# Chunk-select attention and a squared-relu FFN on one core: ones first, split transposes, codes by DMA, an earlier FFN start

## The chip, the cores and the metric

One core of one Trainium2 chip. The metric is the time of one execution in device microseconds (us). The kernel before took 318.02 us, the median of three runs (317.7 to 319.29).

## The reference

Attention over 4 batches, 8 heads, 768 positions of 64 elements, in which each query sees only the six chunks of 32 keys that have the highest upper bounds; its output, as 3072 tokens of 512, goes through an FFN.

```python
k_min = np.min(k_chunks, axis=3)          # chunks of 32 keys, 24 of them
k_max = np.max(k_chunks, axis=3)
ub = np.sum(np.maximum(q[:, :, :, None, :] * k_min[:, :, None, :, :],
                       q[:, :, :, None, :] * k_max[:, :, None, :, :]), axis=-1)
ub = np.where(causal, ub, -1000000000.0)
top_chunks = np.argsort(ub, axis=-1)[..., -top_k:]      # top_k = 6
scores = scale * np.matmul(q, k.transpose(0, 1, 3, 2))
mask = sel & (pos[:, None] >= pos[None, :])             # selected chunk and causal
attn = softmax(np.where(mask, scores, -1e9))
x = (attn @ v) as 3072 tokens x 512
h = np.maximum(x @ w_in, 0.0)                           # 512 x 2048
out = h * h @ w_out                                     # 2048 x 512
```

## The kernel before, in words

The work is cut into 32 slots: batch, half of its positions (384), pair of heads. Half-batch hb is slots 4 hb to 4 hb + 3; slots 0 to 3 are the first half of batch 0, slots 4 to 7 its second half. A half of kind 0 attends to its own 384 keys, one of kind 1 to all 768. For each slot s the program issues these steps, and one step of a slot stands between steps of its neighbours so that each engine's list (made in program order) is interleaved by hand:

- **T(s)** (step_T, L181): for half-batches 0 to 2, PE transposes the pair's keys and queries (L193) into one PSUM tile; ScalarE (ACT) makes relu(-q) and relu(q) (qr, L197, L198), VectorE (DVE) the chunk minima and maxima of the keys (extrema, L170 to L172, into kbd) and copies keys and queries to the tile kq (place, L213). From half-batch 3 on, DMA transposes on SP's queue do this (tr, place_dma); DVE makes the relus (L235, L236) and step_K the extrema of a half-batch, as a tree of pairwise minima or maxima (L252). step_P picks the way.
- **U(s)** (step_U): upper bounds ub as matmuls of qr with kbd (L280), the eight largest by MAX8 (L287), and a comparison that marks the chunks not selected (L288).
- **V(s)** (step_V): PE transposes the marks (qt, L304, L316); copies put them beside the queries (L309, L310, L320, L321). The keys' side of kq holds a large negative one-hot code of each key's chunk, written once per batch tile and half by codes (L141); a marked chunk thus gets a large negative score.
- **E(s)** (step_E): scores ps (L334), exp on ScalarE (L339), the causal mask of the diagonal blocks on GpSimd (POOL, affine_select, L343).
- **F(s)** (step_F): outputs po = e times v with a column of ones for the sum (L359), its reciprocal (L368), x (L369).
- **X(hb)** (step_X): x transposed (by PE, L385, for hb 0, 1 and the last; by DMA otherwise), then sixteen FFN units "up" (ffn_up: ph, L411; relu ht, L418; square h, L420) and twelve units "down" (ffn_down: py, L430) of the half-batch before are put in a queue. fill and f1 take units from it between the steps of later slots; quota says how many a slot takes.

Loads from HBM are issued by POOL (load_n L84, load_0 L91, load_v L96, w_in L453, w_out L458): half-batch 0's keys and queries and half of V at the start, the others at the end of a slot by the table later (at, go). The keys and queries of head pair 0 come by SP and ACT into staged tiles (L105), are cast by DVE and ACT (L177, L179) and are the first that PE transposes. POOL's list is in order, and loads and masks share it. The loads take eight semaphores, DMASW0 to DMASW7, in turn, and a load waits until the load eight before it has landed.

V's tile vn holds the ones (L132 for batch tile 0, in clear for tile 1). PSUM pools: psS three banks (ps), psF two (ph and T of slots 0 to 5), psY one (py and T of slots 6 to 9), psA two (att: ub, qt, po, pt and T of slots 10, 11).

The start reads:

```python
nc.vector.memset(qn0[:, :, :, 3, :], 0.0)
nc.vector.memset(vn[0][:, :, :, D:D + 1], 1.0)      # L132
...
step_cast()
go(-1, 99)
step_P(0)
```

Of the kernel before, what the change touches and what calls it, by code (L numbers as in the profile page):

```python
# [32 lines left out]
def kernel(  # L33
# [175 lines left out]
    def place(s, h, copy):  # L209
        b, half, p = slots[s]  # L210
        x = st[s]["tkq"]
        n = 1 if s < NP else 2
        copy(kqs[b % 2][h][QROW[h]:QROW[h] + D, p, 2 * half:2 * half + n, :],  # L213
             x[D * h:D * h + D, 0:n, :])
# [44 lines left out]

    def step_P(s):  # L260
        hb = s // NP
        if hb >= ON_PE:
# [1 line left out]
        elif s < NP + 2:
            step_T(s, psF, "ph")
        elif s < 2 * NP + 2:
            step_T(s, psY, "py")
        else:
            step_T(s, psA, "att")
# [235 lines left out]
    nc.vector.tensor_scalar_mul(
        oneh.rearrange("p (c j) -> p c j", j=CH),
        ident[0:D, 0:NC].unsqueeze(2).to_broadcast([D, NC, CH]), OFFSEL)
    place(0, 1, nc.scalar.copy)
# [3 lines left out]
    step_P(1)  # L512
    for s in range(NP):
# [11 lines left out]
        if s == NP - 1:
            step_F(s, 0)
            step_F(s, 1)
            early.close()
            late = ctx.enter_context(tc.tile_pool(name="late", bufs=2))
            step_X(0, True)  # L530
            fill(1, True)
        step_V(s + 1, True)
        step_P(s + 2)
        go(s, 99)
    for s, (b, half, p) in enumerate(slots):
# [14 lines left out]

        f1()
# [77 lines left out]
```

## Time and profile before

| | us |
|---|---|
| median of the runs (317.7, 318.02, 319.29) | 318.02 |
| the profiled execution, own time | 319.25 |
| its span in the profile | 317.6 |
| PE busy | 261.5 (82%) |
| ScalarE (ACT) busy | 180.5 (57%) |
| VectorE (DVE) busy | 173.5 (55%) |
| GpSimd (POOL) busy | 100.5 (32%) |

The profiled execution lies 1.65 above its span and 1.23 above the median. Busy time is a sum over the whole span; where time is lost is read from the timeline and from what ended each idle stretch ("[3.36 <-DVE nsel L288]": idle for 3.36 us until VectorE's line 288 was done). PE's own idle time is 317.6 - 261.5 = 56.1 us, and the page's slices show it mostly in the first fifth.

### The profile page before, as it was taken

Reading aid. Unit: us, or ns where it says so; the run is one execution under the profiler, and the core shown is the slowest. Engines: PE = TensorE matmul, PEld = TensorE weight load, DVE = VectorE, ACT = ScalarE, POOL = GpSimd, SP = SyncE. Lnnn points to the kernel's source line nnn. Section 1 sums busy time; section 2 is a strip of 40 time slices with the busy share of each in tenths; the row PEclk is TensorE's granted clock in tenths of the full one; section 3 lists DMA queues with packets and bytes.
Section 4 is the critical chain, followed back from the end, with each engine's and each line's share of the span. In section 5 each row is a group of like instructions: output and inputs, shape, how many; then the busy total and the mean of one; then the engine's idle time right before and its main releaser. Section 6 shows DMA issues by size and latency. Waiting matters only on the chain.

```text
span 317.6 us, 6256 instructions
## 1 busy us (share of the span) xinstructions
PE 261.5 (82%) x2284; PEld 161.2 (51%) x2284; DVE 173.5 (55%) x637; ACT 180.5 (57%) x387; POOL 100.5 (32%) x142
## 2 busy tenths in 40 slices
PE   0147584978598796989997989989979999999994
PEld 0035452656454464656554556655545666655541
DVE  1176558788667752576348525764476455242321
ACT  2046825687466474776564866776556767744300
POOL 8309526965434132442331314511121111000000
PEclk9999998799799999999999999999999999999999
DMA  9997999999958289699698199993650300000011
GB/s 111 166 78 49 78 180 180 115 105 106 120 38 128 53 83 138 53 192 138 92 139 153 54 148 86 136 162 78 109 133 36 83 2 35 33 35 34 33 68 66
DMA packets 109567, 30.36 MB, mean 96 GB/s; under 512 B 99808, under 2 KB 106464, under 8 KB 109536
## 3 DMA queue, kind: packets, MB, share of 16 engines
q0 software_dynamic: 77280, 13.44, 61.0%
q1 hardware_dynamic: 31456, 16.33, 22.8%
q8 instruction: 18, 0.29, 0.4%
q10 hardware_dynamic: 800, 0.20, 0.3%
q14 instruction: 13, 0.11, 0.1%
HBM read 27.26 MB, written 6.29 MB: 106 GB/s over the span
## 4 chain that ended last, share of the span: by engine, by line
PE 56%; DVE 19%; ACT 9%; issue 7%; DMA 6%; SPq 1%; POOL 1%; ACTq 0%; POOLq 0%; DVEq 0%
PE py L430 21%; PE ph L411 19%; PE ps L334 7%; DVE km L252 5%; PE po L359 4%; DMA xT<-x 4%; ACT e L339 3%; DMA w_in<-in_moe_w_in_dram 2%; DVE kq L213 2%; DVE h L420 2%; SPq L395 1%; DVE km L170 1%; PE ub L280 1%; ACT ht L418 1%; DVE km L171 1%
## 5 line engine op out<-in xcount | busy, mean ns | idle before, releaser
L339 ACT ACTIVATE e<-ps 128x512 bf16<-128x512 f32 x192 | 96.6, 550 | 25.9 <-PE ps L334 25.0
L411 PE MATMUL ph<-xT,w_in 128*128 128x384 bf16 x512 | 104.1, 330 | 6.7 <-DMA xT<-x 4.2
L430 PE MATMUL py<-w_out,h 128*128 128x512 bf16 x384 | 96.6, 379 | 0.0
L420 DVE TENSOR_TENSOR h<-ht 128x384 bf16<-128x384 bf16 x128 | 50.8, 401 | 82.5 <-ACT ht L418 82.3
L418 ACT ACTIVATE ht<-ph 128x384 bf16<-128x384 f32 x124 | 61.1, 496 | 53.6 <-PE ph L411 51.8
L343 POOL TENSOR_SCALAR_AFFINE_SELECT e<-e 128x384 bf16<-128x384 bf16 x64 | 33.9, 531 | 166.7 <-ACT e L339 166.6
L411 PEld LDWEIGHTS <-w_in 128*128 128x128 bf16 x512 | 47.5, 99 | 38.7 <-issue 8.1
L334 PE MATMUL ps<-kq 128*128 128x384 bf16 (+2 forms) x320 | 60.2, 294 | 2.1 <-ACT e L339 1.9
L430 PEld LDWEIGHTS <-h 128*128 128x128 bf16 x384 | 35.7, 98 | 31.3
L334 PEld LDWEIGHTS <-kq 128*128 128x128 bf16 x320 | 28.4, 102 | 16.7 <-issue 1.6
L359 PEld LDWEIGHTS <-e 128*128 128x128 bf16 x672 | 27.2, 100 | 8.8 <-issue 2.3
L359 PE MATMUL po<-vn,e 128*128 128x65 bf16 x672 | 28.8, 198 | 1.7 <-DVE r L368 1.0
L280 PE MATMUL ub<-kbd,qr 128*128 128x48 bf16 (+1 forms) x160 | 9.8, 182 | 14.0 <-DVE qr L235 7.5
L287 DVE MAX8 m<-ub 128x8 f32<-128x24 f32 (+1 forms) x160 | 16.6, 169 | 7.1 <-PE ub L280 7.0
L84 POOL DMA_DIRECT2D kn<-in_k_dram x21 | 18.7, 891 | 0.0
L84 POOL DMA_DIRECT2D qn<-in_q_dram x21 | 18.6, 891 | 0.0
L369 DVE TENSOR_TENSOR x<-po,r 128x384 bf16<-128x384 f32 x32 | 17.8, 557 | 1.1
L193 PE MATMUL tkq<-ident,kn 128*128 128x128 bf16 x36 | 5.5, 281 | 14.0 <-DVE kn L177 14.0
L280 PEld LDWEIGHTS <-qr 128*128 128x128 bf16 x160 | 7.9, 99 | 17.0 <-DVE qr L235 8.7
L436 ACT COPY ob<-py 128x512 f32<-128x512 f32 x18 | 10.7, 593 | 8.5 <-PE py L430 8.3
L316 PE MATMUL qt<-ident,nsel 128*128 128x128 bf16 x72 | 9.1, 229 | 6.7 <-DVE nsel L288 6.7
L170 DVE TENSOR_REDUCE km<-tkq 128x12 bf16<-128x384 bf16 x12 | 6.7, 557 | 14.1 <-ACT qr L198 13.4
(64 smaller groups left out, 191.7 us busy)
## 6 DMA issues: line engine op xcount, KB each, us to landing
out_dram<-ob SPq DMA_DIRECT2D x24, 256.0 KB, 2.2
kq<-kqT SPq DMA_DIRECT2D x10, 384.0 KB, 6.7
vn<-in_v_dram POOLq DMA_DIRECT2D x8, 384.0 KB, 7.5
kn<-in_k_dram POOLq DMA_DIRECT2D x21, 128.0 KB, 4.7
qn<-in_q_dram POOLq DMA_DIRECT2D x21, 128.0 KB, 5.6
w_in<-in_moe_w_in_dram POOLq DMA_DIRECT2D x4, 512.0 KB, 7.6
w_out<-in_moe_w_out_dram POOLq DMA_DIRECT2D x2, 1024.0 KB, 14.0
kn<-in_k_dram POOLq DMA_DIRECT2D x3, 96.0 KB, 3.8
```

The costliest lines, as they stand in the source:

```text
L84: nc.gpsimd.dma_start(out=t.rearrange("p (h d) -> p h d", d=D), in_=(q if n == "q" else k)[b, :, 128 * j:128 * (j + 1)] .rearrange("h p d ...
L280: nc.tensor.matmul(ub[:, j - j0], lhsT=st[s]["qr"][:, w, 128 * j:128 * (j + 1)], rhs=kbds[b % 2][:, p, w, :, 0:ncs], start=False, stop=(j ...
L287: nc.vector.max(out=m8[:, j, hh, :], in_=ub[:, j - j0, hh, :])
L334: nc.tensor.matmul(ps[:, at:at + 128 * m], lhsT=kqs[b % 2][hh][:, p, 2 * (j // HT), 128 * (j % HT):128 * (j % HT + 1)], rhs=qc(s, hh)[:, c ...
L339: nc.scalar.activation(e[:, 512 * n + lo:512 * n + hi], ps[:, lo:hi], ACT.Exp, scale=float(scale))
L343: nc.gpsimd.affine_select(out=d, in_=d, compare_op=ALU.is_ge, fill=0.0, base=0, channel_multiplier=-1, pattern=[[0, 3], [1, 128]])
L359: nc.tensor.matmul(po[:, hh, i, :], lhsT=t["e"][hh][:, c:c + 128], rhs=vn[b % 2][:, 2 * p + hh, j, :], start=(j == 0), stop=(j == iq))
L369: nc.vector.tensor_mul(x[:, :, 128 * p:128 * (p + 1)].rearrange("p j (h d) -> p h j d", h=2), po[:, :, :, 0:D], r.to_broadcast([128, 2, HT ...
L411: nc.tensor.matmul(ph[:, 0:HB], lhsT=w_in[:, ki, 128 * f:128 * (f + 1)], rhs=xT[:, ki, :], start=(ki == 0), stop=(ki == NKI - 1))
L418: nc.scalar.activation(ht, ph[:, 0:HB], ACT.Relu)
L420: nc.vector.tensor_mul(h, ht, ht)
L430: nc.tensor.matmul(py[t], lhsT=h2[hb, f][:, 128 * t:128 * (t + 1)], rhs=w_out[:, f, :], start=(f == 0), stop=(f == NFI - 1))
```

## The change

1. The ones of both V tiles and the zeros of nsel are written by DVE ahead of everything else that it does at the start; the two zero stripes of kq tile 1 are written by DVE at slot 1 and no longer by POOL.
2. kq is one tile per batch parity, not one per head, so that V(s) in slots 0 to 3 is one DVE copy of both heads. In the other slots both copies are DVE's (before, ScalarE made the second one in halves of kind 0).
3. step_T is cut in two: transposes into separate PSUM tiles for keys and queries (different pools for slots 0 to 9) and step_T2 with relus, extrema and placing. For slots 0 to 5 the transposes stand a pair ahead, before F and V of the earlier slot. For slots 4 to 11 DVE places the keys and ScalarE the queries.
4. Codes of (tile 0, half 1) and (tile 1, both halves) are written by six DMAs on SP's queue, not by ScalarE (slot 1) and POOL (slots 4, 5). ScalarE makes the one-hot tile first of all.
5. Loads: half-batch 1's keys and queries and the second half of V right at the start, then all of w_in, half-batch 2, w_out, V of batch 1.
6. step_K: minima at the second slot of a half-batch, maxima at the third (before, both at the third).
7. The FFN starts in slot 4, behind E(4,0): F(3), X(0) and the first units; of half-batch 0's relus every second is DVE's (before, every fourth).

```diff
-    kqs = [[consts.tile([128, NP, 4, HB], BF16, tag=f"kq{i}_{h}", name="kq") for h in range(2)]
-           for i in range(2)]
+    kqs = [consts.tile([128, 2, NP, 4, HB], BF16, tag=f"kq{i}", name="kq") for i in range(2)]
...
+    for i in range(2):
+        nc.vector.memset(vn[i][:, :, :, D:D + 1], 1.0)
     ident = consts.tile([128, 128], BF16, tag="ident")
...
-    nc.vector.memset(vn[0][:, :, :, D:D + 1], 1.0)
+    for i in range(3):
+        nc.vector.memset(nsel[i], 0.0)
...
+    def step_T2(s):
+        b, half, p = slots[s]
+        t = st[s]
         qr = t["qr"] = work.tile([128, 2, HB], BF16, tag="qr", bufs=3, name="qr")
         c = 128 * (1 - half)
-        nc.scalar.activation(qr[:, 0, c:], x[:, 1, c:], ACT.Relu, scale=-1.0)
-        nc.scalar.activation(qr[:, 1, c:], x[:, 1, c:], ACT.Relu)
-        extrema(x[:, 0, :], s)
-        t["tkq"] = x
-        place(s, 0, nc.vector.tensor_copy)
+        nc.scalar.activation(qr[:, 0, c:], t["q"][:, c:], ACT.Relu, scale=-1.0)
+        nc.scalar.activation(qr[:, 1, c:], t["q"][:, c:], ACT.Relu)
+        extrema(t["k"], s)
         if s >= NP:
-            place(s, 1, nc.vector.tensor_copy)
+            place(s, "k", nc.vector.tensor_copy)
+            place(s, "q", nc.scalar.copy)
...
+        step_T(s, *((F, Y) if s < NP + 2 else (Y, A) if s < 2 * NP + 2 else (A, A)))
+        if s >= NP + 2:
+            step_T2(s)
...
-            nc.vector.tensor_copy(qc(s, 0), qt[:, 0])
-            nc.scalar.copy(qc(s, 1), qt[:, 1])
+            nc.vector.tensor_copy(kqs[b % 2][:, :, p, 2 * half + 1, :], qt)
...
-        if hb == 0 and f % 4 == 3:
+        if hb == 0 and f % 2:
...
+    for x in load_half(1):
+        at(-1, *x)
+    at(-1, load_v, 0, 4, 8)
+    for g in range(4):
+        at(0, load_w_in, 512 * g, 512 * g + 512)
+    at(0, codes, 0, 1, nc.sync.dma_start)
+    at(1, clear)
+    for x in load_half(2):
+        at(1, *x)
     for g in range(2):
-        at(-1, load_w_in, 512 * g, 512 * g + 512)
-    at(-1, load_v, 0, 4, 8)
-    at(0, clear)
-    for i, x in enumerate(load_half(1)):
-        at(i // 3, *x)
-    for g in range(2, 4):
-        at(2, load_w_in, 512 * g, 512 * g + 512)
+        at(2, load_w_out, 8 * g, 8 * g + 8)
+    for half in range(2):
+        at(2, codes, 1, half, nc.sync.dma_start)
     for g in range(2):
-        at(3, load_w_out, 8 * g, 8 * g + 8)
-    at(1, codes, 0, 1, nc.scalar.copy)
-    at(4, codes, 1, 0, nc.gpsimd.tensor_copy)
-    at(5, codes, 1, 1, nc.gpsimd.tensor_copy)
-    for x in load_half(2):
-        at(4, *x)
-    for g in range(2):
-        at(5, load_v, 1, 4 * g, 4 * g + 4)
+        at(3, load_v, 1, 4 * g, 4 * g + 4)
...
+        if s == NP:
+            for n in range(hf):
+                step_E(s, 0, n)
+            step_F(s - 1, 0)
+            step_F(s - 1, 1)
...
+            step_X(0, True)
+            quota[0] = 3
         f1()
...
         if ON_PE - 1 <= hb < 2 * B - 1:
-            if p == 2:
-                step_K(hb + 1, 0)
-                step_K(hb + 1, 1)
+            if p == 1 or p == 2:
+                step_K(hb + 1, p - 1)
```

How the order moves, in two places. First DVE's list at the start of the program, before, with what each row waits for; kn0 is the key tile of half-batch 0, stage the staged loads, and DMAHW and DMASW are semaphores of loads:

```order
L130 MEMSET qn_79 128x12x32
L131 MEMSET qn_79 128x12x32
L132 MEMSET vn_73 128x48 [waits DMASW6_49]
L177 CAST kn0_85<-stage_92 128x3x128 [waits DMAHW3_49,DMAHW1_49]
L170 TENSOR_REDUCE km_152<-tkq_142 128x12 [waits PE_49,Activation_49]
```

and DVE's list at the same place now:

```order
L109 MEMSET vn_73 128x48
L109 MEMSET vn_74 128x48
L118 MEMSET cmask_110 128x72
...
L134 MEMSET nsel_87 128x192
L176 CAST kn0_83<-stage_90 128x3x128 [waits DMAHW3_49,DMAHW1_49]
L169 TENSOR_REDUCE km_166<-tk_155 128x12 [waits PE_49]
```

The ones of V no longer stand between the other constants and the cast, and no longer wait for a load of V (DMASW6).

Second, POOL's list from the loads at the end of slot 1 to slot 3, before; e are the masks, two a slot, here of slots 2 and 3:

```order
L84 DMA qn_342<-in_q_dram 128x8x64 [waits DMASW7_49]
L343 AFFINE_SELECT e_346<-e_346 128x3x128 [waits Activation_49]
L343 AFFINE_SELECT e_355<-e_355 128x3x128 [waits Activation_49]
L453 DMA w_in_135<-in_moe_w_in_dram 128x4x512 [waits DMASW0_49]
L453 DMA w_in_135<-in_moe_w_in_dram 128x4x512 [waits DMASW1_49]
L343 AFFINE_SELECT e_421<-e_421 128x3x128 [waits Activation_49,Pool_49]
L343 AFFINE_SELECT e_430<-e_430 128x3x128 [waits Activation_49,Pool_49]
L458 DMA w_out_136<-in_moe_w_out_dram 128x8x512 [waits DMASW2_49]
L458 DMA w_out_136<-in_moe_w_out_dram 128x8x512 [waits DMASW3_49]
```

and now, from the last loads of half-batch 2 on:

```order
L83 DMA qn_352<-in_q_dram 128x8x64 [waits DMASW5_49]
L83 DMA qn_354<-in_q_dram 128x8x64 [waits DMASW6_49]
L83 DMA qn_356<-in_q_dram 128x8x64 [waits DMASW7_49]
L353 AFFINE_SELECT e_358<-e_358 128x3x128 [waits Activation_49,Pool_49]
L353 AFFINE_SELECT e_367<-e_367 128x3x128 [waits Activation_49,Pool_49]
L468 DMA w_out_138<-in_moe_w_out_dram 128x8x512 [waits DMASW0_49]
L468 DMA w_out_138<-in_moe_w_out_dram 128x8x512 [waits DMASW1_49]
L353 AFFINE_SELECT e_440<-e_440 128x3x128 [waits Activation_49,Pool_49]
L353 AFFINE_SELECT e_449<-e_449 128x3x128 [waits Activation_49,Pool_49]
```

Loads of half-batch 2 and w_out have moved ahead of the masks of slots 2 and 3. Counted eight back in the new list of loads, DMASW5 stands for the second half of V, DMASW6 and 7 for the first and the second w_in load, DMASW0 and 1 for the third and the fourth.

## Rows read from the trace of the kernel before

**Rows 1.** The page, part 4: the chain that ended last, share of the span by line.

```profile
PE py L430 21%; PE ph L411 19%; PE ps L334 7%; DVE km L252 5%; PE po L359 4%; DMA xT<-x 4%; ACT e L339 3%; DMA w_in<-in_moe_w_in_dram 2%; DVE kq L213 2%; DVE h L420 2%; SPq L395 1%; DVE km L170 1%; PE ub L280 1%; ACT ht L418 1%; DVE km L171 1%
```

**Rows 2.** Timeline, 0 to 20: start, length, engine, line, operation [idle before <-releaser].

```profile
5.71 0.86 POOL L91 DMA_DIRECT2D qn<-in_q_dram  x1
6.53 1.46 POOL L96 DMA_DIRECT2D vn<-in_v_dram  x1
13.35 0.60 DVE L177 CAST kn<-stage 128x384 bf16<-128x384 f32 x1 [10.41 <-issue]
...
19.81 1.23 PE L334 MATMUL ps<-kq 128*128 128x384 bf16 x5
```

**Rows 3.** DMA issues of 6.5 to 7.9 and of 26 to 27: KB, us to landing.

```profile
vn<-in_v_dram POOLq DMA_DIRECT2D x1, 384.0 KB, 6.7
qn<-in_q_dram POOLq DMA_DIRECT2D x1, 96.0 KB, 3.8
...
kn<-in_k_dram POOLq DMA_DIRECT2D x1, 128.0 KB, 3.5
```

**Rows 4.** Timeline, 26 to 62, of POOL, PE and DVE.

```profile
26.40 2.65 POOL L84 DMA_DIRECT2D kn<-in_k_dram  x3
...
35.91 0.52 POOL L343 TENSOR_SCALAR_AFFINE_SELECT e<-e 128x384 bf16<-128x384 bf16 x1 [0.88 <-ACT e L339]
36.45 0.34 PEld L193 LDWEIGHTS <-qn 128*128 128x128 bf16 x2 [0.40 <-DMA qn<-in_q_dram]
...
41.02 1.78 POOL L458 DMA_DIRECT2D w_out<-in_moe_w_out_dram  x2
41.70 0.82 PE L359 MATMUL po<-vn,e 128*128 128x65 bf16 x12 [1.04 <-DVE r L368]
...
45.70 0.53 PE L316 MATMUL qt<-ident,nsel 128*128 128x128 bf16 x3
46.63 0.81 PE L411 MATMUL ph<-xT,w_in 128*128 128x384 bf16 x4
...
50.45 3.12 POOL L141 COPY kq<-oneh 64x1536 bf16<-64x1536 bf16 x2
50.83 2.94 DVE L420 TENSOR_TENSOR h<-ht 128x384 bf16<-128x384 bf16 x2
...
54.91 0.50 PE L316 MATMUL qt<-ident,nsel 128*128 128x128 bf16 x3 [3.36 <-DVE nsel L288]
...
56.59 1.49 PE L411 MATMUL ph<-xT,w_in 128*128 128x384 bf16 x4
...
57.87 1.06 PE L334 MATMUL ps<-kq 128*128 128x384 bf16 x4
```

**Rows 5.** Timeline, 62 to 100: PE before the transposes of x of half-batch 1.

```profile
84.03 0.77 PE L385 MATMUL pt<-ident,x 128*128 128x128 bf16 x6 [2.86 <-DVE x L369]
```

**Rows 6.** Waits of PE: us in total, times, longest.

```profile
PE ub L280 <- DVE qr L235: 7.5, 5, 1.7
...
PE ub L280 <- DVE kbd L172: 6.5, 5, 2.0
```

**Rows 7.** Windows: us, PE, PEld, DVE, ACT, POOL busy, granted clock, DMA share, GB/s.

```profile
39.00:42.00 3.00, 1.57 (x25) 1.37 (x25) 2.80 (x12) 0.53 (x2) 1.75 (x4) 1.00 1.24 205
56.00:58.00 2.00, 2.00 (x12) 1.32 (x11) 0.62 (x2) 1.71 (x4) 2.00 (x3) 0.50 1.62 129
62.00:64.00 2.00, 1.56 (x17) 0.89 (x15) 1.93 (x10) 1.84 (x5) 2.00 (x2) 1.00 0.26 17
```

**Rows 8.** DMA issues of 133 to 140 and of 63 to 64; the page's median of query loads.

```profile
vn<-in_v_dram POOLq DMA_DIRECT2D x1, 384.0 KB, 7.5
qn<-in_q_dram POOLq DMA_DIRECT2D x2, 128.0 KB, 9.3
...
vn<-in_v_dram POOLq DMA_DIRECT2D x1, 384.0 KB, 6.3
...
qn<-in_q_dram POOLq DMA_DIRECT2D x21, 128.0 KB, 5.6
```

More of the change, by code (lines that the diff above doesn't have):

```diff
@@ L140, in codes @@
         for h in range(2):
-            copy(kqs[i][h][SROW[h]:SROW[h] + D, :, 2 * half, :],
+            copy(kqs[i][SROW[h]:SROW[h] + D, h, :, 2 * half, :],
                  oneh[:, HB * half:HB * half + HB].unsqueeze(1).to_broadcast([D, NP, HB]))
     def clear():
-        nc.gpsimd.memset(vn[1][:, :, :, D:D + 1], 1.0)
-        for i in range(3):
-            nc.gpsimd.memset(nsel[i], 0.0)
         for h in range(2):
-            nc.gpsimd.memset(kqs[1][h][SROW[h]:SROW[h] + D, :, 1, 0:128], 0.0)
+            nc.vector.memset(kqs[1][SROW[h]:SROW[h] + D, h, :, 1, 0:128], 0.0)
     w_in = consts.tile([128, NKI, DFF], BF16, tag="w_in")
@@ L179, in step_cast, with step_T @@
         nc.scalar.copy(qn0[:, :, 0, 1:3, :], staged[1])
-    def step_T(s, pool, tag):
+    def step_T(s, kp, qp):
         b, half, p = slots[s]
         t = st.setdefault(s, {})
-        x = pool.tile([128, 2, HB], BF16, tag=tag, name="tkq")
-        for n in range(2):
+        for n, (pool, tag) in enumerate((kp, qp)):
+            if kp is qp and n:
+                x = t["k"][1]
+            elif kp is qp:
+                x = pool.tile([128, 2, HB], BF16, tag=tag, name="tkq")
+                t["k"], x = (x[:, 0], x[:, 1]), x[:, 0]
+                t["q"] = t["k"][1]
+            else:
+                x = pool.tile([128, HB], BF16, tag=tag, name="t" + "kq"[n])
+                t["kq"[n]] = x
             for j in range(HT):
@@ L207, in pack, with place @@
                               n0[1][:, :, p, :])
-    def place(s, h, copy):
+    def place(s, n, copy):
         b, half, p = slots[s]
[L211 to L214, printed above, removed]
+        for h in range(2):
+            copy(kqs[b % 2][QROW[h]:QROW[h] + D, h, p, 2 * half + "kq".index(n), :],
+                 st[s][n][D * h:D * h + D])
     tT = {}
@@ L225, in place_dma @@
             nc.sync.dma_start(
-                out=kqs[hb // 2 % 2][h][QROW[h]:QROW[h] + D, :, 2 * (hb % 2):2 * (hb % 2) + 2, :],
+                out=kqs[hb // 2 % 2][QROW[h]:QROW[h] + D, h, :,
+                                     2 * (hb % 2):2 * (hb % 2) + 2, :],
                 in_=half_T(hb)[D * h:D * h + D])
@@ L258, in step_K @@
                 km, hmask[:, w, h, :].unsqueeze(1).to_broadcast([128, NP, 12]))
+    F, Y, A = (psF, "ph"), (psY, "py"), (psA, "att")
     def step_P(s):
-        hb = s // NP
-        if hb >= ON_PE:
+        if s // NP >= ON_PE:
             relus(s)
[L264 to L269, printed above, removed]
+            return
+        step_T(s, *((F, Y) if s < NP + 2 else (Y, A) if s < 2 * NP + 2 else (A, A)))
+        if s >= NP + 2:
+            step_T2(s)
     def step_U(s):
@@ L294, in qc, with step_V @@
         b, half, p = slots[s]
-        return kqs[b % 2][h][:, p, 2 * half + 1, :]
-    def step_V(s, act=False):
+        return kqs[b % 2][:, h, p, 2 * half + 1, :]
+    def step_V(s):
         b, half, p = slots[s]
@@ L320, in step_V @@
         nc.vector.tensor_copy(qc(s, 0)[0:D, c:], qt[0:D, c:])
-        (nc.scalar.copy if act else nc.vector.tensor_copy)(
+        nc.vector.tensor_copy(
             qc(s, 1)[D:128, c:], qt[D:128, c:])
@@ L335, in step_E @@
                 ps[:, at:at + 128 * m],
-                lhsT=kqs[b % 2][hh][:, p, 2 * (j // HT), 128 * (j % HT):128 * (j % HT + 1)],
+                lhsT=kqs[b % 2][:, hh, p, 2 * (j // HT), 128 * (j % HT):128 * (j % HT + 1)],
                 rhs=qc(s, hh)[:, c:c + 128 * m], start=True, stop=True)
@@ L500, in go @@
                 later[s].pop(0)()
+    nc.scalar.mul(
+        oneh.rearrange("p (c j) -> p c j", j=CH),
+        ident[0:D, 0:NC].unsqueeze(2).to_broadcast([D, NC, CH]), OFFSEL)
     step_cast()
@@ L504 @@
     step_P(0)
[L505 to L508, printed above, removed]
+    step_T2(0)
+    place(0, "k", nc.scalar.copy)
+    step_P(1)
     step_U(0)
@@ L511 @@
     step_V(0)
-    step_P(1)
+    step_T2(1)
     for s in range(NP):
@@ L518 @@
         if s + 1 < NP:
-            place(s + 1, 1, nc.scalar.copy)
+            place(s + 1, "k", nc.scalar.copy)
             pack(s + 1)
         step_E(s, 1, 1)
+        step_P(s + 2)
         if s:
@@ L524 @@
             step_F(s - 1, 1)
[L525 to L533, printed above, removed]
+        step_V(s + 1)
+        step_T2(s + 2)
         go(s, 99)
@@ L538 @@
         hb = s // NP
-        act = half == 0
         nb = len(BANKS[half])
@@ L549, in f1 @@
                 fill(1, True)
+        if s == NP:
[3 more added lines that the diff above has]
+            step_F(s - 1, 1)
+            early.close()
+            late = ctx.enter_context(tc.tile_pool(name="late", bufs=2))
+            step_X(0, True)
+            quota[0] = 3
         f1()
@@ L556 @@
             step_X(hb - 1, hb == 2)
-        for n in range(hf):
-            step_E(s, 0, n)
+        if s > NP:
+            for n in range(hf):
+                step_E(s, 0, n)
         f1()
@@ L575 @@
         if s + 1 < NS:
-            step_V(s + 1, act)
+            step_V(s + 1)
         go(s, 99)
```

4 lines of the change are left out of this document (3 added, 1 removed).

## The prediction

> **What bounds the kernel now.** I read the chain of work that ended last first: its largest shares are TensorE's [rows 1], so from the middle on the kernel ends when PE's list ends, and time is lost where PE stands idle. I then went along PE's timeline for places where it waits and read who released it. Three stretches matter. (a) The start. The last of the six key and query loads of half-batch 0 is issued at 5.71 and takes 3.8, so it lands at 9.5; the first half of V, issued at 6.53, takes 6.7 and lands at 13.2 [rows 2, 3]. The cast of the staged keys starts only at 13.35 [rows 2], just behind that landing: the ones (L132) share V's tile, stand ahead of the cast on VectorE (DVE), and wait for the load. (b) From 41.70, the outputs F(3) of slot 3, to 57.87, the scores E(5,0) of slot 5: 16.17 us for little more than one slot, with PE idle for 3.36 before 54.91 while DVE's two squares took 2.94 beside a codes copy of 3.12 on POOL [rows 4]. (c) From slot 5 on, waits for DVE: 6.5 for key extrema, 7.5 for the relus behind step_K, 2.86 before a transpose of x [rows 5, 6].
>
> I count two steps of time: when F(3) can run, and what lies between F(3) and the end.
>
> **When F(3) runs.** With the ones first, the cast needs only the staged loads, and slots 0 to 3 begin many us sooner. But the start is not the bound then. POOL issues all the loads in order; each waits for the load eight before it to land (its eight DMASW semaphores), and masks of e stand behind these waits. In the changed order the two w_out issues stand ahead of slot 3's masks and wait for the third and the fourth w_in load; F(3) needs the masks. In the old order all loads those waits name had landed long before. So I add up the loads, one after another:
> - key and query loads of half 0 landed: 9.5; first V half: 13.2, that is 3.7 later [rows 2, 3];
> - six 128 KB loads. Three key and three query loads were issued from 26.40; the first took 3.5 and landed at 29.9, and PE was waiting for the last one until 36.45, so five took 6.55, 1.31 each [rows 3, 4]: 13.2 + 6 x 1.31 = 21.1;
> - second V half, 3.7 like the first: 24.8;
> - four w_in loads of 512 KB at 205 GB/s [rows 7], 2.5 each: 34.8;
> - one w_out issue, 1.78 / 2 = 0.9 [rows 4], and a mask, 0.52 [rows 4]: 36.2.
>
> To this comes what the codes cost, now six transfers of 192 KB on SP's queue. They wait for nothing but the one-hot tile, so all of them run among these loads at the start. The trace has no codes transfer. The nearest rows are the pair of placements of 384 KB each, also SBUF to SBUF on SP's queue: beside such a pair a V load took 7.5, against 6.3 without it, and two query loads 9.3, against a median of 5.6 [rows 8]: a delay of 1.2 or of 3.7. The codes are 1152 KB against 768 KB, one and a half times: 1.8 to 5.6. The other bound is nothing, if they fill time in which the loads leave engines free. I take the middle of the two measured values, 3.7. F(3) then runs at 39.9, against 41.70: **1.8 gained**, bounds 0 and 5.5.
>
> The Trainium skill, DMA: Bandwidth & Descriptors, in the section "Issuing engines are not separate DMA queues", speaks against moving work to SP's queue: DMAs from any issuing engine run on the same sixteen engines and interleave. The rows on the pair agree (9.3 against 5.6). The same page, "Where 436 GB/s comes from", gives a ceiling of 435 GB/s; at that the codes would cost an estimated 2.7 in place of 3.7, and the sum below would be 1.0 larger.
>
> **From F(3) to E(5,0).** 16.17 before [rows 4]. (1) The codes copies leave POOL and ScalarE; the squares no longer run beside one, and PE's idle time of 3.36 goes. (2) Code transposes V(4) and natural transposes T(5), 46.63 - 45.70 = 0.93, and E(4,0), half of 1.06 since that row ran at half clock (the granted clock was 0.50 there, the lower level, 1.2 GHz [rows 7]), are done before F(3) while PE waits for the masks: 0.93 + 0.53 = 1.5. (3) One FFN unit fewer stands before E(5,0): 0.81 at full clock, 1.49 at half [rows 4], 1.15 between. It goes to the end of half-batch 1, where PE waits 2.86 [rows 5] and which covers it; without that cover it costs 0.81 again. Together **6.0 gained**, bounds 3.4 ((1) alone) and 7.5 (also part of the slow clock).
>
> **Slots 5 to 8.** Key extrema no longer wait for ScalarE's relus of the queries, since keys and queries now lie in different PSUM banks; PE's wait behind extrema (L172) is 6.5 in 5 waits, 1.3 each [rows 6]. I count 1.7 of it in these slots. The wait of 2.86 before the transposes of x [rows 5] falls by about 1.0, as DVE has no query copies to place. Against that stands a second FFN relu in four on DVE, inside its idle time. **2.7 gained**, bounds 0 and 4.
>
> **step_K.** Minima and maxima of a half-batch now come one slot apart. PE waits 7.5 in 5 waits for the relus queued behind them [rows 6], one wait for each of half-batches 3 to 7. The split halves the block on DVE. I take all 7.5 as gone, less one block in slot 9, where the minima now stand ahead of extrema that PE needs: DVE's tree is 5% of the chain, 15.9 us, over ten trees 1.6 each [rows 1]. **5.9 gained**, bounds 0 (each half still delays one relu) and 7.5.
>
> Other edits cost nothing I can see: one copy of 128x2x384 in place of two, and memsets moved from POOL to DVE's start, are covered by the loads that gate F(3); if that cover goes, they cost a copy each.
>
> **Sum.** 1.8 + 6.0 + 2.7 + 5.9 = 16.4. The profiled execution took 319.25, so 302.9 by its own time; that one lies 1.2 above the median of the runs, 318.02, and the forecast stands against the median: 301.6. About 0.5%, 1.6 us, is what a measurement of this kernel can tell from no change.
>
> **The rivals.**
> - The codes cost the loads nothing. F(3) runs at 36.2: 3.7 more gained, 297.9. For: the V load lost only 1.2 beside a pair. Against: 9.3 against 5.6. Chance 0.20.
> - POOL's queue doesn't hold the masks, since loads overlap and land sooner. Slots 0 to 3 then set the pace. T(1), ahead of U(0) on PE, waits for the loads at 9.5; with 3.1 for U(0), V(0) and the copies, an estimate, E(0) starts at 12.6. F(3) came 21.9 after E(0) (41.70 - 19.81 [rows 2, 4]), of which the codes copies on ScalarE go, some 3 like those on POOL: 12.6 + 19 = 31.6, 8.3 earlier than forecast, 293.3. Against: 205 GB/s at 39 to 42 [rows 7] is a rate that loads alone reached. Chance 0.08. The opposite failure, a first cast that still comes late, changes little: F(3) waits for the loads anyway.
> - The split of step_K gives nothing back, or the new PSUM rotation (transposes take banks of the FFN and of att) takes as much: 5.9 less, 307.5. For: bounds of 0 to 7.5, and the pools have one or two buffers each. Chance 0.20.
> - Slower: PE's clock. Before 54.91 PE idled 3.36, and in 56 to 58 the granted clock was 0.50 [rows 4, 7]; the same FFN unit took 1.49 against 0.81, a group of scores 1.06 against some 0.53. In the changed kernel PE idles at the masks of slots 2 and 3, just before the FFN starts. If the clock stays at 1.2 GHz through slots 4 to 8, each slot pays 4 units x 0.68 and 4 groups x 0.5, 4.7; four and a half slots pay 21, and the time is 323, slower. It decides from 16.4 / 4.7, three and a half slots. Against: the clock was back at 1.00 in 62 to 64 [rows 7]. Chance 0.04. The Trainium skill, TensorE: Matmul & The Clock Gate, section "HAM oscillation — how this bites in real kernels", describes a kernel whose PE falls back to the lower clock at each wait for a DMA; the fall in 56 to 58 agrees that idling costs clock, and no row here shows it lasting over slots.
>
> **How the numbers follow.** My forecast 0.45, with a range of its own from 299 to 306; the rivals 0.20, 0.08, 0.20 and 0.04; 0.03 for what I don't see, shared between no change and faster. The range reaches from between the first two rivals, 295.5, to beyond the third, 309, and leaves out some 0.15. All but the clock rival and a part of the rest are faster by far over 0.5%: faster 0.94, same 0.02, slower 0.04.
>
> **What would show it.** First transposes of PE near 5 and the two ones first on DVE; POOL's loads waiting on DMASW and the masks of slots 2 and 3 behind them; F(3) near 40, released by POOL; no codes copy on POOL or ScalarE; E(5,0) near 50 (57.87 - 1.8 - 6.0) with no PE idle over 2 before it; the wait of ub for the relus of queries (L235 before) near 2 in place of 7.5. I am wrong in the first step if F(3) runs before 37 or after 43, in the second if F(3) to E(5,0) takes over 13, in the last if ub still waits 5 or more for the relus.

## The result, and the profile after

The changed kernel took 301.71 us (median of four runs, 299.96 to 304.01) against 318.65 (median of four, 317.7 to 322.51; three of them gave the 318.02 above): a ratio of 0.948, 95% interval 0.939 to 0.958. The forecast was 301.6. The profiled execution took 300.71, near the low end of its runs, with a span of 299.0, 18.6 less than before. From the page of the changed kernel: the span, busy times, the granted clock in 40 slices, and the chain by line.

```profile
span 299.0 us, 6267 instructions
PE 257.0 (86%) x2284; PEld 157.2 (53%) x2284; DVE 175.3 (59%) x655; ACT 179.6 (60%) x385; POOL 92.4 (31%) x132
...
PEclk9999559999999999999999999999999999999999
...
PE py L440 22%; PE ph L421 21%; PE ps L344 8%; DMA kn<-in_k_dram 7%; PE po L369 5%; DMA xT<-x 4%; DVE km L264 4%; ACT e L349 3%; SPq L405 2%; DVE h L430 2%; ACT kq L224 1%; PE ub L291 1%; DVE x L379 1%; PE qt L326 1%; ACT ht L428 1%
```

PE's busy time fell by only 4.5; the rest, 14.1, was idle time. Its timeline, with DVE's and POOL's rows that set it, to be read beside [rows 2, 4]:

```profile
1.05 0.31 DVE L109 MEMSET vn<- 128x48 bf16 x2 [1.05 <-PEq L625]
4.92 0.50 PE L200 MATMUL tk<-ident,kn 128*128 128x128 bf16 x3 [4.92 <-DVE kn L176]
11.79 0.29 PE L200 MATMUL tk<-ident,kn 128*128 128x128 bf16 x1 [4.54 <-DMA kn<-in_k_dram]
15.89 1.23 PE L344 MATMUL ps<-kq 128*128 128x384 bf16 x5 [1.74 <-DVE kq L320]
...
31.77 0.88 POOL L83 DMA_DIRECT2D qn<-in_q_dram  x1 [1.66 <-DMA w_in<-in_moe_w_in_dram]
33.24 0.98 PE L369 MATMUL po<-vn,e 128*128 128x65 bf16 x12 [2.67 <-POOL e L353]
34.34 0.89 POOL L468 DMA_DIRECT2D w_out<-in_moe_w_out_dram  x1 [0.68 <-DMA w_in<-in_moe_w_in_dram]
36.88 0.88 POOL L468 DMA_DIRECT2D w_out<-in_moe_w_out_dram  x1 [1.65 <-ACT e L349]
37.76 1.00 POOL L353 TENSOR_SCALAR_AFFINE_SELECT e<-e 128x384 bf16<-128x384 bf16 x2
38.35 0.98 PE L369 MATMUL po<-vn,e 128*128 128x65 bf16 x12 [1.89 <-POOL e L353]
47.28 0.60 PE L344 MATMUL ps<-kq 128*128 128x384 bf16 x4
...
73.68 0.49 PE L344 MATMUL ps<-kq 128*128 128x384 bf16 x3
79.83 0.18 PE L287 MATMUL ub<-cmask,ident 128*128 128x48 bf16 x1 [1.13 <-ACT kq L224]
89.43 0.18 PE L287 MATMUL ub<-cmask,ident 128*128 128x48 bf16 x1 [2.64 <-ACT kq L224]
```

The chain of the forecast stands there: the ones at 1.05, the first transposes at 4.92; then PE waits for masks at F(2) and F(3), behind loads that wait on POOL. (The row at 36.88 names ScalarE's e; in POOL's list this issue waits only for the fourth w_in load.) A wait that the forecast does not have stands ahead of them: 4.54 before 11.79, for a key load of half-batch 0 that now runs beside the code transfers (5.6 in two waits; 3.0 in e1 below, which has no code transfers). F(3) runs at 38.35, E(5,0) at 47.28, E(8,0) at 73.68. The last two rows are the upper bounds waiting for a PSUM bank, 3.8 in all; before, this wait was 1.06, once, ahead of 98.65.

Waits of PE in the changed kernel (us in total, times, longest), and two windows of the granted clock:

```profile
PE po L369 <- POOL e L353: 4.6, 2, 2.7
PE ub L287 <- ACT kq L224: 3.8, 2, 2.6
...
PEld L291 <- DVE qr L247: 1.9, 5, 0.5
...
PE ub L291 <- DVE qr L247: 0.5, 2, 0.3
```

```profile
30.00:33.00 3.00, 0.57 (x6) 0.30 (x3) 0.61 (x5) 2.43 (x6) 1.33 (x3) 0.50 1.24 206
44.00:48.00 4.00, 3.75 (x39) 2.56 (x37) 3.68 (x15) 3.90 (x9) 0.52 (x1) 1.00 1.25 207
```

Of the wait for the relus behind step_K, 7.5 [rows 6], 0.5 is left on PE and 1.9 on its weight loads. The clock was at the lower level (0.50) from 30 on, around the masks of slots 2 and 3, and back at 1.00 by 44; in the 3 us before 30 PE had been busy for 1.57.

Where the 18.6 came from, by the start of the outputs F(s) of a slot on PE. Each row is the one profiled execution of that kernel, so a stretch also holds what the clock did in that execution; the last column is the median of all its runs:

| kernel | F(3) | F(4) | F(8) | F(12) | F(31) | median us |
|---|---|---|---|---|---|---|
| before | 41.70 | 60.01 | 88.97 | 124.16 | 276.59 | 318.65 |
| changed | 38.35 | 48.37 | 77.19 | 112.41 | 257.92 | 301.71 |
| e1 codes on engines | 33.16 | 44.27 | 72.89 | 109.20 | 255.00 | 297.73 |
| e2 loads behind masks | 33.16 | 45.33 | 74.14 | 110.50 | 256.35 | 298.44 |
| e3 trees together | 37.88 | 48.75 | 77.58 | 116.69 | 268.85 | 312.22 |
| e4 queries by DVE | 39.09 | 49.20 | 79.66 | 115.74 | 260.73 | 306.00 |
| e5 fewer relus by DVE | 39.33 | 49.61 | 76.66 | 114.62 | 261.25 | 300.50 |
| e6 before, ones first | 32.84 | 51.15 | 80.13 | 116.45 | 269.75 | 310.24 |
| e7 codes later | 36.07 | 45.66 | 74.36 | 111.43 | 259.33 | 300.70 |
| e8 e7 and e2 | 28.23 | 39.65 | 68.48 | 106.46 | 253.28 | 296.09 |
| e9 queries ahead | 39.62 | 49.72 | 78.52 | 112.31 | 257.74 | 303.29 |
| e10 combined | 29.80 | 41.97 | 69.02 | 102.99 | 250.71 | 291.80 |
| e11 FFN in slot 3 | 39.08 | 52.36 | 80.16 | 114.01 | 260.23 | 303.75 |
| e12 before, split | 41.62 | 58.86 | 90.08 | 125.98 | 272.13 | 313.02 |

Changed against before: 3.35 up to F(3), 8.29 to F(4), 0.14 in F(4) to F(8), nothing in F(8) to F(12), 6.92 in F(12) to F(31).

### The profile page after: what moved, and what is told of

It reads as the page before. It is cut to its first block, busy times and chain, and to the rows that moved or that the text cites. A ratio compares the mean times of both kernels' runs of the same rounds, so it can differ in the third digit from the quotient of the medians.

```text
span 299.0 us, 6267 instructions
## 1 busy us (share of the span) xinstructions
PE 257.0 (86%) x2284; PEld 157.2 (53%) x2284; DVE 175.3 (59%) x655; ACT 179.6 (60%) x385; POOL 92.4 (31%) x132
## 4 chain that ended last, share of the span: by engine, by line
PE 60%; DVE 15%; DMA 11%; ACT 6%; POOL 3%; issue 2%; SPq 2%; ACTq 0%; POOLq 0%
PE py L440 22%; PE ph L421 21%; PE ps L344 8%; DMA kn<-in_k_dram 7%; PE po L369 5%; DMA xT<-x 4%; DVE km L264 4%; ACT e L349 3%; SPq L405 2%; DVE h L430 2%; ACT kq L224 1%; PE ub L291 1%; DVE x L379 1%; PE qt L326 1%; ACT ht L428 1%
## 5 line engine op out<-in xcount | busy, mean ns | idle before, releaser
L421 PE MATMUL ph<-xT,w_in 128*128 128x384 bf16 x512 | 102.8, 328 | 4.1 <-DMA xT<-x 3.4
L430 DVE TENSOR_TENSOR h<-ht 128x384 bf16<-128x384 bf16 x128 | 47.2, 369 | 74.2 <-ACT ht L428 73.5
L428 ACT ACTIVATE ht<-ph 128x384 bf16<-128x384 f32 x120 | 59.3, 495 | 45.8 <-PE ph L421 43.7
L344 PE MATMUL ps<-kq 128*128 128x384 bf16 (+2 forms) x320 | 57.7, 284 | 5.3 <-DVE kq L320 3.8
L369 PE MATMUL po<-vn,e 128*128 128x65 bf16 x672 | 27.8, 196 | 4.6 <-POOL e L353 4.6
L369 PEld LDWEIGHTS <-e 128*128 128x128 bf16 x672 | 26.2, 99 | 9.8 <-POOL e L353 5.3
L83 POOL DMA_DIRECT2D qn<-in_q_dram x21 | 18.6, 897 | 3.8 <-DMA w_in<-in_moe_w_in_dram 2.7
L200 PE MATMUL tk<-ident,kn 128*128 128x128 bf16 x30 | 4.5, 261 | 10.5 <-DMA kn<-in_k_dram 5.6
L330 DVE COPY kq<-qt 64x384 bf16<-64x384 bf16 (+1 forms) x28 | 8.9, 318 | 6.0 <-PE qt L326 5.8
L95 POOL DMA_DIRECT2D vn<-in_v_dram x8 | 11.9, 1493 | 0.1
L326 PEld LDWEIGHTS <-nsel 128*128 128x128 bf16 x72 | 5.8, 99 | 11.0 <-DVE nsel L299 7.3
```

Source lines behind the costliest of these rows:

```text
L83: nc.gpsimd.dma_start(out=t.rearrange("p (h d) -> p h d", d=D), in_=(q if n == "q" else k)[b, :, 128 * j:128 * (j + 1)] .rearrange("h p d ...
L326: nc.tensor.matmul(qt[:, 128 * j:128 * (j + 1)], lhsT=nsel[s % 3][:, j].rearrange("p h d -> p (h d)"), rhs=ident, is_transpose=True, start ...
L344: nc.tensor.matmul(ps[:, at:at + 128 * m], lhsT=kqs[b % 2][:, hh, p, 2 * (j // HT), 128 * (j % HT):128 * (j % HT + 1)], rhs=qc(s, hh)[:, c ...
L369: nc.tensor.matmul(po[:, hh, i, :], lhsT=t["e"][hh][:, c:c + 128], rhs=vn[b % 2][:, 2 * p + hh, j, :], start=(j == 0), stop=(j == iq))
L421: nc.tensor.matmul(ph[:, 0:HB], lhsT=w_in[:, ki, 128 * f:128 * (f + 1)], rhs=xT[:, ki, :], start=(ki == 0), stop=(ki == NKI - 1))
L430: nc.vector.tensor_mul(h, ht, ht)
```

## The experiments

**e1, codes on the engines again.** (e1 to e5, e7, e9 and e11 are the changed kernel with one edit each; e6 and e12 are the kernel before with one edit each; e8 and e10 put edits together.)

```diff
-    at(0, codes, 0, 1, nc.sync.dma_start)
...
-        at(2, codes, 1, half, nc.sync.dma_start)
+    at(1, codes, 0, 1, nc.scalar.copy)
+    at(4, codes, 1, 0, nc.gpsimd.tensor_copy)
+    at(5, codes, 1, 1, nc.gpsimd.tensor_copy)
```

> The changed kernel with the codes written by ScalarE (slot 1) and POOL (slots 4, 5) again, not by DMA. My theory: the six code transfers cost the loads of the start some 2 us (in the changed kernel the last w_in load lands near 36.9, against 34.8 worked out without codes), so without them F(3) comes earlier, at 36 to 37 in place of 38.35; but POOL's copies of 3 us stand beside VectorE's squares again, and F(3) to F(4) grows from 10.0 to about 13. Together 303 to 305. Rival, the codes cost the loads nothing: F(3) stays at 38 or later (the copy on ScalarE), and the time is 305 or more. Rival, the idle time of 3.36 was not due to the copies: F(3) to F(4) stays near 10, and the time is 299 to 301.

It took 297.73 (ratio to before 0.937, 0.930 to 0.943), less than any of the three theories had, and less than the changed kernel: its four runs, 297.05 to 299.56, all lie below the other's, 299.96 to 304.01. Timeline of e1:

```profile
31.69 0.87 POOL L468 DMA_DIRECT2D w_out<-in_moe_w_out_dram  x1 [1.65 <-ACT kq L224]
33.16 0.83 PE L369 MATMUL po<-vn,e 128*128 128x65 bf16 x12 [1.16 <-POOL e L353]
36.82 3.02 POOL L143 COPY kq<-oneh 64x1536 bf16<-64x1536 bf16 x2
37.94 0.59 DVE L430 TENSOR_TENSOR h<-ht 128x384 bf16<-128x384 bf16 x1 [2.66 <-ACT ht L428]
39.28 0.78 DVE L430 TENSOR_TENSOR h<-ht 128x384 bf16<-128x384 bf16 x1
44.27 1.12 PE L369 MATMUL po<-vn,e 128*128 128x65 bf16 x30
```

The last w_out issue moved from 36.88 to 31.69 and F(3) from 38.35 to 33.16: the transfers cost the loads 5.2. DMA issues of 10.5 to 13, the query loads of half-batch 1, in the changed kernel and then in e1:

```profile
qn<-in_q_dram POOLq DMA_DIRECT2D x3, 128.0 KB, 11.4
```

```profile
qn<-in_q_dram POOLq DMA_DIRECT2D x3, 128.0 KB, 5.7
```

Beside the codes these loads took twice as long. F(3) to F(4) grew by 1.1, not 3, and most of that goes with the clock: PE was busy for 10.20 against 9.27 with as many matmuls, at a mean granted clock of 0.69 against 0.74. The first third of the copies (36.82 to 37.94) fell into time in which VectorE waited for ScalarE. The two squares beside them took 0.59 and 0.78 against 0.36 without a copy (e6 below has one), and 2.94 for two in [rows 4]. The Trainium skill, SBUF — State Buffer, section "SBUF: two separate sides", says that a VectorE operation with two SBUF inputs and a GpSimd one that reads SBUF shut each other out for a whole instruction. The rows agree: the squares of [rows 4] ended 0.2 after the copies, and so did each of the two of e1.

**e2, loads of half-batch 2, w_out and V of batch 1 behind the masks.**

```diff
-        at(1, *x)
+        at(3, *x)
...
-        at(2, load_w_out, 8 * g, 8 * g + 8)
+        at(4, load_w_out, 8 * g, 8 * g + 8)
...
-        at(3, load_v, 1, 4 * g, 4 * g + 4)
+        at(5, load_v, 1, 4 * g, 4 * g + 4)
```

> The changed kernel with the loads of half-batch 2 at slot 3, w_out at slot 4 and V of batch 1 at slot 5, so that no load waits ahead of the masks of slots 2 and 3. My theory: F(2) and F(3) are held by loads that wait in POOL's queue; without them F(3) runs near 32 in place of 38.35 and the time falls by 4 to 6, to 296 to 298. Rival, the landing of w_in itself holds the FFN: F(3) is early but its first units wait, and less than 2 is gained, 300 to 302. Rival, the loads now come too late for the slots behind (T(8) or F(8) wait): no gain or a loss.

298.44 (0.938, 0.931 to 0.945), 0.4 above what was expected. F(3) ran at 33.16 with no wait for POOL, so the masks behind waiting loads were what held it. Only 3.0 of the 5.2 was left at F(4). PE's timeline of e2:

```profile
33.16 0.54 PE L369 MATMUL po<-vn,e 128*128 128x65 bf16 x12
...
35.86 0.82 PE L395 MATMUL pt<-ident,x 128*128 128x128 bf16 x6 [1.82 <-DVE x L379]
```

VectorE, which has extrema and key copies of slot 5 ahead of x in its list, is late next.

**e3, both trees of step_K in one slot again.**

```diff
-            if p == 1 or p == 2:
-                step_K(hb + 1, p - 1)
+            if p == 2:
+                step_K(hb + 1, 0)
+                step_K(hb + 1, 1)
```

> The changed kernel with both trees of step_K at the third slot of a half-batch, as before. My theory: the split is worth what the intervals between outputs show, 1.4 to 2.2 at each of half-batches 3 to 7, so the time rises by 6 to 8, to 308 to 310, and PE waits some 7 for the relus of queries. Rival, the gain behind slot 8 came from elsewhere (the copies of queries on ScalarE, separate banks): under 2 more, 303 or less.

312.22 (308.6 to 312.86), 10.5 above the changed kernel, more than expected. PE's waits of e3:

```profile
PE ub L291 <- DVE qr L247: 9.5, 5, 2.4
```

Against the changed kernel 3.9 is lost from F(8) to F(12) and 6.6 behind. Windows of F(8) to F(12), in the changed kernel and then in e3:

```profile
77.19:112.41 35.22, 29.07 (x236) 16.75 (x235) 22.79 (x87) 21.29 (x48) 9.21 (x14) 1.00 0.65 88
```

```profile
77.58:116.69 39.11, 31.98 (x235) 17.73 (x234) 22.89 (x87) 21.96 (x48) 9.29 (x15) 0.91 0.69 91
```

Of the 3.9, 2.9 is PE's busy time for as many matmuls, at a mean granted clock of 0.91 against 1.00: not idle time, but longer matmuls.

**e4, queries placed by VectorE**, `place(s, "q", nc.vector.tensor_copy)`.

> The changed kernel with the queries of slots 4 to 11 placed by VectorE, not by ScalarE. In the changed kernel F(4) to F(6) take 7.9 and 7.8 a slot against 7.2 and 7.3 before. My theory: ScalarE's two copies of 0.96 a slot, ahead of the exps and relus that the next scores and squares wait for, lengthen each slot; without them slots take 7.0 to 7.4 and the time falls by 1 to 2.5, to 299 to 301. Rival, VectorE with its extra relu is the bound: 0.7 a slot more, 304 to 305. Third, neither: the same time.

306.0 (303.5 to 306.17). My theory fell: F(4) to F(6) took 15.2 against 15.7, and F(7) to F(8), with the transposes of x, 9.0 (70.68 to 79.66) against 7.0; 1.3 of that 2.0 is PE's busy time (6.25 against 4.96) at a mean granted clock of 0.81 against 1.00. ScalarE's copies are the better place by the whole time, but not by slots 4 and 5.

**e5, fewer relus on VectorE**, `f % 4 == 3` in place of `f % 2`.

> The changed kernel with every fourth relu of half-batch 0's FFN on VectorE, as before, not every second. The runs so far show that slots 4 to 6 take 7.6 to 7.9 each wherever the queries are placed, against 7.2 to 7.3 before the change. My theory: VectorE is the bound of these slots (idle under 1 us in each), and one relu of 0.56 a slot less makes each 0.4 to 0.6 shorter: F(4) to F(7) falls from 21.8 to about 20.5, the time by 1 to 2. Rival, ScalarE, which takes the relu at 0.49, is the bound: the slots get longer by as much, 302 to 303. Third, a loop through both: no change within 1.

300.5 (299.31 to 304.16) against 301.71: not to be told apart as a whole. The stretch itself shows the edit: F(4) to F(7) took 20.0 (49.61 to 69.64) against 21.8 in the changed kernel, and again 20.0 (41.97 to 61.99) in e10, which has the edit, against 21.8 (39.65 to 61.45) in e8, which does not; the granted clock was 1.00 in all four. What became shorter is PE's wait for VectorE's marks (nsel) between F(4) and F(7): 1.68, 1.52 and 1.07 in e8, 1.08, 0.93 and 0.48 in e10, together 1.8 less. The first of each, e8 and then e10:

```profile
44.94 0.34 PE L326 MATMUL qt<-ident,nsel 128*128 128x128 bf16 x3 [1.68 <-DVE nsel L299]
```

```profile
46.66 0.34 PE L329 MATMUL qt<-ident,nsel 128*128 128x128 bf16 x3 [1.08 <-DVE nsel L302]
```

So what PE waits for here is on VectorE. Its load as such is not the bound: in e4 it was busy for 1.7 more from F(4) to F(7), and the stretch took 21.5.

**e6, the kernel before with the ones first** (the line L132 moved ahead of the identity).

> The kernel before with one edit alone: the ones of V's first tile written ahead of everything else on VectorE. My theory: the first scores then start near 13 in place of 19.81, but the loads of half-batch 1, which are issued behind the masks of slots 0 and 1, follow earlier too, so F(3) comes 4 to 6 earlier (36 to 38 in place of 41.70), and all of it stays to the end: 313 to 315. Rival, the start is covered by the loads (the FFN's first units wait for w_in, as the chain of waits of the kernel before has it): under 1.6 gained, 317 to 319.

310.24 (0.975, 0.970 to 0.981), more than expected: one line is worth some 8 us. Timeline of e6, DVE and PE:

```profile
1.06 0.10 DVE L109 MEMSET vn<- 128x48 bf16 x1 [1.06 <-PEq L613]
4.22 0.55 DVE L177 CAST kn<-stage 128x384 bf16<-128x384 f32 x1 [1.08 <-DMA stage<-in_k_dram]
...
32.84 0.82 PE L359 MATMUL po<-vn,e 128*128 128x65 bf16 x12 [1.04 <-DVE r L368]
37.61 0.36 DVE L420 TENSOR_TENSOR h<-ht 128x384 bf16<-128x384 bf16 x1 [2.66 <-ACT ht L418]
46.05 0.50 PE L316 MATMUL qt<-ident,nsel 128*128 128x128 bf16 x3 [3.37 <-DVE nsel L288]
```

F(3) came 8.9 earlier, at 32.84, and so 5.5 earlier than in the changed kernel. What holds that one back is its load order and its code transfers: with the transfers later and the loads behind the masks (e8) its F(3) is at 28.23. F(3) to F(4) stayed at 18.3, with its idle time of 3.37.

**e7, codes by ScalarE's queue at the end of slots 1 and 3**, not SP's at the start.

> The changed kernel with the six code transfers issued by ScalarE's queue at the end of slots 1 and 3 in place of SP's at the start. My theory: what the codes cost is that they run beside the loads of the start; issued later they cost those loads less, and there are no copies on an engine: F(3) at 33 to 35 in place of 38.35 and the time 295 to 298, at most as long as with the copies on ScalarE and POOL (297.7). Rival, the transfers hold the loads back wherever they run: F(3) at 37 or later and 300 or more.

300.70 (299.1 to 302.12): F(3) at 36.07 lies between the two theories, and the time is the rival's. Beside w_in the transfers cost the loads less than beside the small ones, but not nothing: e1 had 33.16.

**e8, e7 and e2 together.**

> Both edits together: codes at the end of slots 1 and 3 by ScalarE's queue, and the loads of half-batch 2, w_out and V of batch 1 behind the masks of slots 2 and 3. Each alone had F(3) at about 33. My theory: without both, slots 0 to 3 set the pace from the loads of half-batch 0 on, F(3) runs at 28 to 31, and the time is 293 to 296. Rival, w_in or the loads of half-batch 1 hold it at 33: 297 or more.

296.09 (0.928, 0.923 to 0.933), just outside what was expected (293 to 296). F(3) ran at 28.23, as expected; from there to F(4) no row of PE waits for a load or for POOL.

**e9, queries ahead in slots 10 and 11.**

```diff
+        if s >= 2 * NP + 2:
+            place(s, "q", nc.scalar.copy)
         extrema(t["k"], s)
...
-            place(s, "q", nc.scalar.copy)
+            if s < 2 * NP + 2:
+                place(s, "q", nc.scalar.copy)
```

> The changed kernel with one order turned: for slots 10 and 11, where keys and queries share a PSUM tile, ScalarE places the queries ahead of VectorE's extrema and key copies. In the changed kernel that ScalarE copy waits for VectorE's copy of the keys of the same tile (2.0 and 4.0 us in slots 8 and 9), and PE waits 1.1 and 2.6 for it at the next upper bounds. My theory: this wait is a new one that the change made, and turning the order removes 1.5 to 3 of the 3.8: 298.7 to 300.5. Rival, the extrema then wait for ScalarE, and their upper bounds come as late: no change within 1. Third, worse: 303.

303.29 (300.55 to 305.83), no gain by its runs. PE's waits of e9, and its window of F(8) to F(12):

```profile
PE ub L290 <- DVE kq L227: 3.6, 2, 2.4
```

```profile
78.52:112.31 33.79, 28.32 (x232) 16.74 (x234) 23.91 (x87) 21.12 (x48) 9.29 (x14) 1.00 0.64 89
```

The wait of 3.8 all but stayed and changed its releaser: the bank in psA is held until VectorE's key copies are through. Still, in the profiled execution F(8) to F(12) took 33.8 against 35.2, at a granted clock of 1.00 in both, so the order is worth some 1.4 there; F(3) and F(8) came 1.3 later, and nothing of it is left at F(31) (257.74 against 257.92).

**e10, the four edits of e2, e5, e7 and e9.**

> The four edits together: codes at the end of slots 1 and 3 on ScalarE's queue, half-batch 2, w_out and V behind the masks, every fourth relu on VectorE, queries placed ahead in slots 10 and 11. The first two together gave 296.1. My theory: the relus are worth 1 to 2 in slots 4 to 6 and the order of the queries 1.5 to 3 in slots 8 and 9: 292 to 294.5. Rival, the gains are taken up by the wait for xT in slot 12 (2.25 with the first two): 295 or more.

291.80 (290.21 to 293.52), ratio 0.917, 0.913 to 0.921: faster than the change beyond both intervals, and a little faster than expected. Busy time and clock on its page:

```profile
PE 258.4 (89%) x2257; PEld 160.1 (55%) x2284; DVE 173.1 (59%) x651; ACT 181.0 (62%) x389; POOL 92.1 (32%) x132
...
PEclk9999689999999999999999899999999999999999
```

Of its 4.3 against e8, the relus explain 1.8 in F(4) to F(7). From F(8) to F(12) it took 34.0 against 38.0. Windows of this stretch, e8 and then e10:

```profile
68.48:106.46 37.98, 31.37 (x237) 17.75 (x234) 23.04 (x87) 22.14 (x48) 9.38 (x15) 0.93 0.69 91
```

```profile
69.02:102.99 33.97, 28.33 (x232) 16.72 (x235) 23.91 (x87) 21.13 (x48) 9.26 (x14) 1.00 0.72 99
```

The mean granted clock was 0.93 and 1.00. At 1.00 in both, e9's order gave 1.4; by that estimate the other 2.6 goes along with the clock (see the last section).

**e11, the FFN begun in slot 3 again** (F(3), X(0) and one unit ahead of V(4), and three more in slot 4).

> The changed kernel with the FFN started where it was before: F(3), X(0) and one unit in slot 3, ahead of V(4) and E(4,0). My theory: F(3) stays at 38 (held by POOL's queue), the code transposes and E(4,0) now come after it, and F(3) to F(4) grows from 10.0 by 2 to 4, to 12 to 14: 303 to 306. Rival, the later start is what took the 8.3 out of this stretch: it grows to 16 or more, 308 or more. Third, it doesn't matter: 10 to 11, 301 to 303.

303.75 (301.92 to 304.81), as expected. PE's outputs of slots 3 and 4 in e11:

```profile
39.08 0.98 PE L369 MATMUL po<-vn,e 128*128 128x65 bf16 x12 [4.17 <-POOL e L353]
52.36 1.12 PE L369 MATMUL po<-vn,e 128*128 128x65 bf16 x30
```

F(3) to F(4) took 13.3, 3.3 more than in the changed kernel; 2.3 of it is left at F(31), since F(4) to F(12) took 61.65 against 64.04.

**e12, the kernel before with the split of step_K alone.**

> The kernel before with one edit alone: minima of step_K at the second slot, maxima at the third. The changed kernel lost 10.5 when the split was undone. My theory: each of half-batches 4 to 7 gains 1.4 to 2, half-batch 3 about 1 to 4, so the time falls by 6 to 9, to 309 to 312. Rival, the split is worth 10 only beside the other edits, and little alone: 314 or more.

313.02 (0.981, 0.975 to 0.987), 5.3 less than its own before of 318.28: a little less gained than expected (6 to 9). F(12) to F(31) took 146.15 against 152.43.

## Why the prediction was right, step by step

The time came out to 0.1, and that closeness is luck. By the profiled executions the four terms of the sum were 3.35, 7.24, 0.3 and, from E(8,0) to the end, 7.6, where 1.8, 6.0, 2.7 and 5.9 had been forecast: three too small, one too large. Their sum, 18.5, is that of two single executions; the medians differ by 16.9. What holds F(3), the earlier FFN start and the split of step_K were right as mechanisms; other parts of the second and the third term were not.

**When F(3) runs: 1.8 forecast, 3.35 measured.** That the masks behind waiting loads hold it is shown by e2. The size came from two errors that partly cancelled. Without codes the loads were through by 31.69 (e1), not 34.8. Most of that is the 1.31 for a 128 KB load: it was read from loads that POOL issued one by one (2.65 for three [rows 4]) with no load before them under way, while loads that queue, in e1's window of 14.5 to 17, moved 155 GB/s, 0.85 for each:

```profile
14.50:17.00 2.50, 1.78 (x14) 1.18 (x12) 1.55 (x6) 2.04 (x6) 1.76 (x4) 1.00 2.43 155
```

And the codes cost 5.2, not 3.7, near the upper bound of 5.6. The estimate of 2.7 by the Trainium skill's ceiling of 435 GB/s (DMA: Bandwidth & Descriptors, "Where 436 GB/s comes from") was further off. "The start is not the bound then" holds for the changed kernel only because of its own load order and code transfers (e8).

**From F(3) to E(5,0): 6.0 forecast, 7.24 measured** (16.17 to 47.28 - 38.35 = 8.93). Parts (2) and (3), the later FFN start, were put at 2.65; e11 gives 3.3 at F(4). Part (1) was not borne out. It took the whole 3.36 of PE's idle time for the price of the copies. But two squares without a copy take 0.72, so the copies held them for 2.2 of the 2.94 [rows 4], no more; and with the copies put back (e1) the stretch grows by 1.1, most of it with the clock. What the copies cost in the kernel before, where the squares fall almost wholly beside them, was not tried. Of the 8.3 to F(4), 3.3 is the FFN start, and 5.0 lies in the rest: the missing copies, transposes a pair ahead, separate banks and the relus. How these share it was not tried either.

**Slots 5 to 8: 2.7 forecast, 0.3 measured** (E(5,0) to E(8,0): 57.87 [rows 4] to 84.59, 26.72, before; 47.28 to 73.68, 26.40, now). This is the step that failed, in two of its three parts. First, it counted 1.7 of PE's wait of 6.5 behind the key extrema [rows 6] in these slots, and none of it lies there: the five waits stand before 16.85, 22.28, 27.17, 32.05 and 39.39, all ahead of F(3) at 41.70. The last of them, and E(8,0), in the kernel before:

```profile
39.39 0.40 PE L280 MATMUL ub<-kbd,qr 128*128 128x48 bf16 x6 [1.23 <-DVE kbd L172]
...
84.59 0.84 PE L334 MATMUL ps<-kq 128*128 128x384 bf16 x3
```

Second, "a second FFN relu in four on DVE, inside its idle time", was put at nothing. VectorE had 2.3 us of idle time in the 19.5 from F(4) to F(7) before; still the relus cost 1.8 there (e10 against e8), all of it as PE's wait for VectorE's marks. The third part, the shorter wait before the transposes of x, was right in kind: 2.86 became 1.07. F(7) to F(8) fell by 2.4, of which 1.3 is PE's busy time (6.26 to 4.96) at a mean granted clock of 0.82 before and 1.00 now.

**step_K: 5.9 forecast.** 5.3 alone (e12), 6.9 from F(12) on in the changed kernel, and 10.5 when undone there (e3). Of the 3.9 more that e3 loses between F(8) and F(12), 2.9 goes with a lower granted clock. There the change itself gained nothing (35.19 before, 35.22 now): the split's wait for the relus fell from 1.75 to 0.26, and the wait for the bank of slots 10 and 11 grew from 1.06 to 3.8.

**The rivals.** The rival in which the codes cost nothing fell by e1, the one in which POOL's queue does not hold the masks by the timeline and e2. That the split gives nothing back fell by e12 and e3; that the new PSUM rotation takes as much was half right: it cost the waits of 3.8 for psA. The clock rival's fall came (0.50 in 30 to 33) but ended by 44, early in the FFN's first slot, and did not last over slots.

## What to carry to other kernels

A load that waits for a semaphore on an in-order queue holds everything behind it (here 5.2 us of F(3), e2): before moving loads forward, count which earlier load each one waits for and what stands behind it. Read the duration of loads that will queue from a place where loads queue, not from one where they are issued one by one. A transfer "for nothing" at the start runs beside the loads that gate the start; try each part of a change alone, since here one line is worth 7.7 by itself (e6) and another part cost 4.0 (e1). Before a wait's total is counted as the gain of some slots, look up at which times its single waits stand.

## What the runs showed that I had not expected

Six 192 KB transfers from SBUF to SBUF made 128 KB loads from HBM take 11.4 in place of 5.7. And a wait of PE of 2.6 in slot 9 was followed by a mean granted clock of 0.75 in e1, but of 1.00 in the profiled execution of the changed kernel, which had the same wait, so that a stretch of one execution can differ from another's by the clock alone; windows of the stretch behind it, in the changed kernel and then in e1:

```profile
90.00:94.00 4.00, 3.93 (x26) 2.03 (x24) 3.42 (x13) 3.44 (x10) 1.04 (x2) 1.00 0.46 130
```

```profile
86.00:91.00 5.00, 5.00 (x26) 2.54 (x25) 3.63 (x13) 3.33 (x9) 1.04 (x2) 0.75 0.59 157
```
